# Strict turns between loads and DMA transposes for two batches of a fused attention and mixture-of-experts kernel

## The chip, the core and the metric

The kernel runs on one core of one Trainium2 chip. The metric is the device time of one execution in microseconds. The time before is the median of nine runs. Profiles are one execution each, taken by the hardware profiler; "the span" is the time from the first to the last instruction in it.

Engines as the profile names them: PE is TensorE (PEld its weight loads), DVE is VectorE, ACT is ScalarE, POOL is GpSimd, SP is SyncE. POOL and SP mostly issue DMAs here.

## What is computed

A cosine-weighted linear attention over 8 batches, 8 heads, 576 positions and 64 dimensions, and behind it a layer of 8 experts whose gates are balanced by eight Sinkhorn rounds.

```python
def phi(x, c, s):
    r = np.maximum(x, 0.0)
    return np.concatenate([r * c, r * s], axis=-1)
q_p = phi(q, cos_w, sin_w)
k_p = phi(k, cos_w, sin_w)
kv = np.einsum('bhsf,bhsd->bhfd', k_p, v)
z = np.sum(k_p, axis=2)
num = np.einsum('bhsf,bhfd->bhsd', q_p, kv)
den = np.einsum('bhsf,bhf->bhs', q_p, z)[..., None] + 1e-06
...
logits = x @ w_gate
logits = logits - logits.max()
P = np.exp(logits)
for _ in range(8):
    P /= P.sum(1, keepdims=True) + 1e-09
    P /= P.sum(0, keepdims=True) + 1e-09
    P *= N / E
for e in range(E):
    h = np.maximum(x @ w1[e], 0.0)
    ye = h @ w2[e]
    out += P[:, e:e + 1] * ye
```

Here x is num / den with the heads side by side: 4608 tokens of 512 values.

## The kernel before

The program has two parts. In the first, the attention of the eight batches is woven into the first expert's two matrix products. In the second, the other seven experts follow, in a form with fewer multiplications. The change touches the first part only.

**Blocks and slots.** The first expert's work is cut into blocks j = 0 to 6 of 512 tokens. A block has 16 slots (`NS`). Slots 0 to 7 (`ffn1`) each multiply by one slice of w1 into a bank `h_ps` (two of them) and let ScalarE write the Relu to `hT`. Slots 8 to 15 (`ffn2`) each do half of one row of w2 into `y_ps`, which ScalarE copies to `acc` after every second slot. Behind each slot the program runs what the dictionary `todo` holds for it; `at(j, slot, fn, ...)` puts a step there. Within a slot, steps run in the order in which they were put (lines 668 to 757).

**Attention steps.** In block j, batch b = j + 1 is brought to its end (`sums`, `denominators`, `spread_out`, `numerators`, whose result `xT` the next block reads), and batch b + 1 is prepared:
- `prep_q(b, hk)`: VectorE takes the Relu of a pair of heads' queries in place (`q_ld`), multiplies by the cosines and sines into `q_p` (a pool of three buffers), and, from batch 2 on, SP issues a DMA transpose of `q_p` into one of eight homes: six `q_pT` tiles, a lent piece of `acc_lo`, a lent piece of `acc_hi` (line 361). A batch has four such pairs, hk = 0 to 3.
- `prep_k(b, hk)`: the Relu of the keys in place, on ScalarE in these blocks (line 342).
- `prep_kv(b, hk)`: VectorE multiplies the keys by cosines and sines into `k_p`, and copies v into a home with a column of ones (in `acc_lo`).
- `sums(b, half)`: TensorE multiplies `k_p` with v, 36 matmuls for a half (two pairs).
- `denominators(b)`: TensorE multiplies the turned queries of all four pairs with the key sums; it needs all four transposes.

**Loads.** `load(b, half, names, held_back)` issues one DMA on POOL's queue for each of q, k, v, half a batch each, from 32-bit input to 16-bit tiles (`q_ld`, `k_ld`, `v_ld`, four buffers of each name). With `held_back` it waits for the last VectorE instruction written before it. Six loads bring a batch. The loads of batch 4 are put at slot 12 of block 1, those of batch 5 at slots 11 and 12 of block 2.

**Order.** TensorE, VectorE and ScalarE are wrapped so that each runs its instructions in the written order (`InOrder`, `te`, `ve`, `se`). SP and POOL are not wrapped; the framework places their instructions, and each still issues one after the other. `after(earlier, i)` adds a real wait of i for `earlier`; for a DMA `earlier`, that is its completion. Before the change there is one such wait between loads and transposes: the transpose of (b = 3, hk = 0) waits for the landing of the second half of batch 3's v.

The batches count from zero: the fourth and fifth batch are b = 3 and b = 4. Block 1 prepares b = 3, block 2 prepares b = 4, block 3 prepares b = 5. In the profile TensorE begins block 2 at 66.81 us, block 3 at 87.06 us and block 4 at 106.10 us.

The profile gives line 109 for every operation of the three wrapped engines, so groups there are told apart by their tiles.

Of the kernel before, what the change touches and what calls it, by code (L numbers as in the profile page):

```python
# [25 lines left out]
def kernel(  # L26
# [18 lines left out]
    HK = H // 2  # L45
# [46 lines left out]
    def after(earlier, i):  # L92

        tc.add_manual_dep(
            i.ins,
            earlier.ins.name,
            mybir.DependencyInfo(mybir.DependencyClass.Sync, mybir.DependencyReason.DATA),
            reason="start",
        )
# [81 lines left out]
    with ExitStack() as p1:  # L181
# [11 lines left out]

        loaded = {}
        landing = {}
        sources = {"q": q, "k": k, "v": v}

        def load(b, half, names="qkv", held_back=False):
            for name in names:
                x = ld.tile([P, 2, C, D], F16, name=f"{name}_ld")  # L200
                view = sources[name][b].rearrange("(hk hh) (p c) d -> (hh p) hk (c d)", hh=2, c=C)
                i = nc.gpsimd.dma_start(  # L202
                    out=x[:].rearrange("p hk c d -> p hk (c d)"),
                    in_=view[:, 2 * half : 2 * half + 2],
                )
                if held_back:

                    after(ve.last, i)
                landing[name, b, half] = i
                for i in range(2):  # L210
                    loaded[name, b, 2 * half + i] = x[:, i]
# [20 lines left out]
        for name in "kv":  # L232
            load(0, 0, name)
            load(0, 1, name)
# [111 lines left out]
        def prep_q(b, hk):  # L346

            q16 = loaded.pop(("q", b, hk))
            by_dma = b >= 2
            if by_dma:  # L350
                ve.tensor_scalar(
                    out=q16, in0=q16, scalar1=0.0, scalar2=None, op0=ALU.max
                )
            q_p = qp_pool.tile([P, C, 2, D], F16, name="q_p")
            ve.tensor_tensor(
                out=q_p[:], in0=q16.unsqueeze(2).to_broadcast([P, C, 2, D]),
                in1=cs, op=ALU.mult,
            )
            if by_dma:
                qTs[b, hk] = q_pTs[(b * HK + hk) % len(q_pTs)]  # L360
                turned = nc.sync.dma_start(
                    out=qTs[b, hk], in_=q_p[:].rearrange("p c a d -> p (c a d)"),
                    transpose=True,
                )
                if b == 3 and hk == 0:

                    after(landing["v", b, 1], turned)
            else:
                qps[b, hk] = q_p

# [97 lines left out]
        def sums_made(b, half, kv_ps):  # L468
            kv_sb, zsel = kvs[b]
            W_ = D + 1 if b else D  # L470
            for hh in range(2):
                kv_v = kv_ps[hh][:, 0 : 2 * W_].rearrange("p (hk d) -> p hk d", d=W_)
                se.copy(out=kv_sb[:, 2 * half : 2 * half + 2, hh, :], in_=kv_v[:, :, 0:D])
                if b:
                    ve.tensor_tensor(
                        out=zsel[:, 4 * half + hh : 4 * half + 4 : 2, :],
                        in0=zmask[:, 4 * half + hh : 4 * half + 4 : 2, :],
                        in1=kv_v[:, :, D : D + 1].to_broadcast([P, 2, 32]),
                        op=ALU.mult,
                    )  # L480
# [123 lines left out]
        def at(block, slot, fn, *args):  # L604
            todo.setdefault((block, slot), []).append((fn, args))
# [59 lines left out]
        for hk in range(3):  # L665
            prep_q(1, hk)

        for j in range(B):
            b = j + 1
            if j == 0:  # L670

                def sums_first(half):
                    sums_made(1, half, sums_begun(1, half))

                for hk in range(HK):
                    for i in range(3):
                        at(0, (5, 6, 6, 7)[hk], turn, 1, hk, i, i != 1)
                    if hk == 0:
                        at(0, 5, prep_q, 1, 3)
                    if hk == 2:  # L680
                        at(0, 6, prep_v, 1, 0, se.copy)
                        at(0, 6, prep_v, 1, 2, ve.tensor_copy)
                    if hk == 3:
                        at(0, 7, prep_v, 1, 1, se.copy)
                        at(0, 7, prep_v, 1, 3, ve.tensor_copy)
                for half in range(2):
                    at(0, 7, sums_first, half)
                at(0, 8, denominators, 1)
                at(0, 10, gates, 0)
                for hk in range(HK):  # L690
                    at(0, 11 + hk, attend, 1, hk)
            elif b < B:
                if j == 1:
                    at(0, 13, load, b + 1, 0, "q", True)
                    for hk in range(HK):
                        if hk >= 2:
                            at(j, 0, prep_k, b, hk, False)
                        at(j, 0, prep_kp, b, hk)
                        at(
                            j, (0, 0, 1, 3)[hk], prep_v, b, hk,  # L700
                            (ve.tensor_copy, se.copy)[hk // 2],
                        )
                    for name, half in (("q", 1), ("k", 0), ("k", 1), ("v", 0), ("v", 1)):
                        at(j, 0, load, b + 1, half, name, True)
                    at(j, 3, sums, b, 0)
                    at(j, 5, sums, b, 1)
                elif j == 2:
                    at(j, 0, sums, b, 1)
                else:
                    at(j, 0, prep_kv, b, 2)  # L710
                    at(j, 1, prep_kv, b, 3)
                    at(j, 2, sums, b, 0)
                    at(j, 2, sums, b, 1)
                at(j, 6 if j == 1 else 3 if j == 2 else 4, denominators, b)
                for hk in range(HK):
                    if j == 1:
                        at(j, (9, 10, 12, 13)[hk], attend, b, hk)
                    else:
                        at(j, (7, 8, 10, 11)[hk], spread_out, b, hk)
                if j > 1:  # L720
                    at(j, 9, numerators_of, b, 0, 1)
                    at(j, 13, numerators_of, b, 2, 3)
            if j:
                at(j, 5, gates, j)
            if j == 0:
                for half in range(2):
                    at(j, 3, load, b + 1, half)
                for slot, fn, hk, *args in (
                    (8, prep_q, 0), (11, prep_k, 0), (12, prep_q, 1), (12, prep_k, 1),
                    (13, prep_q, 2), (14, prep_q, 3),  # L730
                ):
                    at(j, slot, fn, b + 1, hk, *args)
            elif b + 1 < B:
                for slot, fn, hk in (
                    (4, prep_q, 0), (5, prep_q, 1), (8, prep_k, 0), (8, prep_q, 2),
                    (9, prep_k, 1), (10, prep_kv, 0), (10, prep_k, 2), (12, prep_q, 3),
                    (12, prep_kv, 1), (12, prep_k, 3), (13, prep_kv, 2), (14, prep_kp, 3),
                    (14, prep_v, 3),
                ) if j == 1 else (
                    (4, prep_q, 0), (5, prep_k, 0), (5, prep_q, 1), (6, prep_k, 1),  # L740
                    (8, prep_q, 2), (8, prep_k, 2), (10, prep_q, 3), (10, prep_k, 3),
                    (11, prep_kv, 0), (14, prep_kv, 1),
                ) if j == 2 else (
                    (3, prep_k, 0), (4, prep_k, 1), (5, prep_q, 0), (6, prep_q, 1),
                    (7, prep_k, 2), (8, prep_q, 2), (10, prep_q, 3), (10, prep_k, 3),
                    (11, prep_kv, 0), (14, prep_kv, 1),
                ):
                    at(j, slot, fn, b + 1, hk, *((se.copy,) if fn is prep_v else ()))
                if j == 1:
                    at(j, 15, sums, b + 1, 0)  # L750
            if j == 1:
                for name in "qkv":
                    for half in range(2):
                        at(j, 12, load, b + 2, half, name, True)
            elif j and b + 2 < B:
                for half in range(2):
                    at(j, 11 + half, load, b + 2, half, "qkv", True)
# [490 lines left out]
    while stream:  # L1248
        _, pair, name = stream.pop(0)
# [32 lines left out]
```

The softmax here doesn't subtract the row's maximum and nothing guards it: scores larger than these inputs give would overflow.

## Time and profile before

| what | value |
|---|---|
| median of nine runs | 978.71 us (977.74 to 979.42) |
| the profiled execution | 978.71 us |
| its span | 977.0 us |
| granted TensorE clock | 1.00 |
| TensorE busy in block 2 (66.81 to 87.06 us) | 18.89 of 20.25 us |
| TensorE busy in block 3 (87.06 to 106.10 us) | 19.04 of 19.04 us |
| a transpose, issue on SP | about 1.3 us |
| a transpose, issue to landing | 3.2 to 9.9 us |
| a load of half a batch, issue on POOL | about 0.72 us |
| median to landing: q, k, v loads | 6.7, 8.7, 9.8 us |

Times in a timeline are from the start of the span. A line has the start, the duration, the engine, the line of the source, the operation, the written and the read tile with their shapes, and the count of merged instructions; in square brackets stands how long the engine was idle just before, and what ended that. For a DMA the duration is that of its issue; when the data has landed is told by the view of DMA issues, in which the last number of a line is the median time from issue to landing.

### The profile page before, as it was taken

What the parts mean: (1) busy time and instruction counts of PE and PEld (TensorE: products, weight loads), DVE (VectorE), ACT (ScalarE), POOL (GpSimd) and SP (SyncE); (2) the same over time, 40 slices, a digit from 0 to 9 for tenths busy, and PEclk for the clock granted to TensorE, in tenths of its full rate; (3) what the DMA queues carried; (4) which work ended last, traced back from release to release, by engine and by line L of the source; (5) the groups of instructions that cost most, each with busy time, mean ns of one, the idle gap of its engine ahead of it and who ended that gap; (6) DMA issues with size and microseconds to landing.
All of it is one profiled execution on the core that took longest, in us unless ns stands there. A gap on an engine that the chain in (4) does not pass through costs nothing.

```text
span 977.0 us, 20236 instructions
## 1 busy us (share of the span) xinstructions
PE 962.5 (99%) x7855; PEld 675.5 (69%) x7855; DVE 808.0 (83%) x1833; ACT 563.6 (58%) x1262; POOL 60.7 (6%) x82
## 2 busy tenths in 40 slices
PE   9999999999999999999999999999999999999997
PEld 6545555457777777777777777777777777777775
DVE  6767775888988887988888887988888888988887
ACT  5766665477776555555555555555555555555551
POOL 6231110010000000000000000000000000000001
PEclk9999999999999999999999999999999999999999
DMA  9999985330104401323103401323103401104435
GB/s 163 184 153 174 152 141 111 68 68 34 42 25 84 77 25 41 64 53 68 34 25 84 77 25 39 65 53 65 38 25 80 81 25 37 38 26 121 127 89 128
DMA packets 80336, 73.54 MB, mean 75 GB/s; under 512 B 33264, under 2 KB 72176, under 8 KB 80240
## 3 DMA queue, kind: packets, MB, share of 16 engines
q0 software_dynamic: 27232, 30.94, 20.2%
q1 hardware_dynamic: 52768, 41.06, 17.3%
q8 instruction: 61, 1.00, 0.4%
q14 instruction: 35, 0.29, 0.1%
q10 hardware_dynamic: 240, 0.26, 0.1%
HBM read 83.12 MB, written 12.98 MB: 98 GB/s over the span
## 4 chain that ended last, share of the span: by engine, by line
PE 88%; DMA 5%; DVE 3%; issue 2%; ACT 1%; POOL 1%; POOLq 0%; ACTq 0%; SPq 0%
PE rows_ps L109 33%; PE h_ps L109 26%; PE p_ps L109 11%; PE copied_ps L109 11%; PE y_ps L109 4%; PE small_ps L109 2%; DMA k_ld<-in_k_dram 1%; DMA w1e<-in_moe_w_dram 1%; DMA w2e<-in_moe_w_dram 1%; DMA acc_hi<-q_p 1%; DVE P_tok L109 1%; DVE colp L109 0%; POOL q_ld L202 0%; DVE rs L109 0%; DVE acc_hi L955 0%
## 5 line engine op out<-in xcount | busy, mean ns | idle before, releaser
L955 DVE SCALAR_TENSOR_TENSOR acc_lo<-rows_ps,P_tok,acc_lo 128x512 f32<-128x512 f32 (+1 forms) x322 | 203.5, 641 | 74.9 <-PE rows_ps L109 74.8
L109 PEld LDWEIGHTS <-H 128*128 128x128 f16 x2080 | 203.1, 98 | 82.5 <-issue 1.2
L891 ACT CAST u<-h_ps 128x384 f16<-128x384 f32 x288 | 137.5, 478 | 131.3 <-PE h_ps L109 131.3
L109 PEld LDWEIGHTS <-w1e 128*128 128x128 f16 x1632 | 157.7, 98 | 67.6 <-issue 5.2
L885 DVE CUSTOM_DVE_ANT_0 H<-p_ps,u 128x384 f16<-128x384 f32 x329 | 181.3, 551 | 6.5 <-PE p_ps L109 6.5
L109 PEld LDWEIGHTS <-hs 128*128 128x128 f16 x1500 | 146.6, 98 | 56.2
L109 PE MATMUL h_ps<-S,w1e 128*128 128x384 f16 x672 | 164.1, 326 | 0.7 <-ACT u L109 0.6
L109 PE MATMUL p_ps<-xT,T 128*128 128x384 f16 x672 | 164.1, 326 | 0.1
L109 PE MATMUL rows_ps<-V,H 128*128 128x256 f16 x1000 | 150.0, 273 | 0.7 <-DVE acc_hi L955 0.7
L109 PE MATMUL rows_ps<-w2e,hs 128*128 128x256 f16 x1000 | 150.0, 273 | 0.0
L109 PE MATMUL h_ps<-xT,w1e 128*128 128x384 f16 (+1 forms) x616 | 148.7, 350 | 0.1
L923 ACT ACTIVATE H<-h_ps 128x384 f16<-128x384 f32 x144 | 70.6, 490 | 95.1 <-PE h_ps L109 95.1
L109 PEld LDWEIGHTS <-T 128*128 128x128 f16 x1008 | 98.4, 98 | 30.2 <-issue 3.6
L109 PE MATMUL rows_ps<-w2e,H 128*128 128x256 f16 (+1 forms) x568 | 92.3, 285 | 0.0
L904 ACT COPY copied_ps<-h_ps 128x384 f32<-128x384 f32 x144 | 67.5, 469 | 35.5 <-PE h_ps L109 35.5
L914 ACT ACTIVATE H<-copied_ps 128x384 f16<-128x384 f32 x144 | 70.8, 492 | 20.4 <-PE copied_ps L109 20.4
L109 PE MATMUL h_ps<-S,T 128*128 128x384 f16 x336 | 81.8, 324 | 0.5 <-ACT copied_ps L109 0.3
L109 PE MATMUL copied_ps<-xT,w1e 128*128 128x384 f16 x336 | 82.1, 326 | 0.0
L109 PE MATMUL copied_ps<-w2e,H 128*128 128x256 f16 x504 | 75.5, 272 | 0.0
L109 PE MATMUL rows_ps<-V,hs 128*128 128x256 f16 x500 | 75.0, 272 | 0.0
L955 DVE SCALAR_TENSOR_TENSOR acc_lo<-copied_ps,P_tok,acc_lo 128x256 f32<-128x256 f32 x126 | 60.2, 478 | 0.6 <-PE copied_ps L109 0.2
L955 DVE SCALAR_TENSOR_TENSOR acc_hi<-rows_ps,P_tok,acc_hi 128x512 f32<-128x512 f32 (+1 forms) x56 | 41.3, 738 | 20.5 <-PE rows_ps L109 19.7
(145 smaller groups left out, 949.9 us busy)
## 6 DMA issues: line engine op xcount, KB each, us to landing
S<-x_saved SPq DMA_DIRECT2D x108, 192.0 KB, 2.4
out_dram<-acc_lo SPq DMA_DIRECT2D x62, 128.0 KB, 2.4
w1e<-in_moe_w_dram POOLq DMA_DIRECT2D x7, 1024.0 KB, 8.8
w2e<-in_moe_w_dram POOLq DMA_DIRECT2D x7, 1024.0 KB, 9.6
q_ld<-in_q_dram POOLq DMA_DIRECT2D x16, 288.0 KB, 6.7
k_ld<-in_k_dram POOLq DMA_DIRECT2D x16, 288.0 KB, 8.7
v_ld<-in_v_dram POOLq DMA_DIRECT2D x16, 288.0 KB, 9.8
x_saved<-S SPq DMA_DIRECT2D x18, 192.0 KB, 1.9
```

The costliest lines, as they stand in the source:

```text
L109: i = getattr(self.engine, name)(*args, **kwargs)
L885: latest = ve._custom_dve(TENSOR_ADD_SAT, out=out, in0=ps[:, 0:TU], in1=t[:], s0=FP32_MAX, s1=0.0)
L891: se.copy(out=t[:], in_=ps[:, 0:TU])
L904: se.copy(out=Y[:, 0:TU], in_=X[:, 0:TU])
L914: se.activation(out=h11, in_=Y[:, 0:TU], func=AF.Relu)
L923: se.activation(out=h12, in_=X[:, 0:TU], func=AF.Relu)
L955: ve.scalar_tensor_tensor(out=a, in0=rows, scalar=P_tok[:, g, self.e : self.e + 1], in1=a, op0=ALU.mult, op1=ALU.add,)
```

## The change

Two kinds of waits are added, and the steps of block 2 get other slots.

- All four transposes of batches 3 and 4 wait for the landing of the second half of their batch's v. Before, only (3, 0) did.
- `turnings` remembers each transpose. The loads of batch 4 wait for the completion of the transpose (3, 3), and those of batch 5 for that of (4, 3), in place of the wait for VectorE's last instruction. The loads of batch 5 are put at slot 14 of block 2 instead of 11 and 12.
- In block 2 the preparation of batch 4 moves: `prep_q` from slots 4, 5, 8, 10 to 6, 7, 9, 14; `prep_k` from 5, 6, 8, 10 to 9, 10, 11, 12; `prep_kv` of pair 0 from 11 to 13; that of pair 1 stays at 14, now behind `prep_q` of pair 3.
- Block 3, which prepares batch 5, and all later blocks keep their slots; so do the loads of batch 6 and 7.

```diff
@@ def load
-        def load(b, half, names="qkv", held_back=False):
+        def load(b, half, names="qkv", held_back=False, behind=None):
...
-                if held_back:
+                if behind is not None:
+
+                    after(turnings[behind], i)
+                elif held_back:
 
                     after(ve.last, i)
@@ def prep_q
-                if b == 3 and hk == 0:
+                if b in (3, 4):
 
                     after(landing["v", b, 1], turned)
+                turnings[b, hk] = turned
@@ the steps of block 2
-                    (4, prep_q, 0), (5, prep_k, 0), (5, prep_q, 1), (6, prep_k, 1),
-                    (8, prep_q, 2), (8, prep_k, 2), (10, prep_q, 3), (10, prep_k, 3),
-                    (11, prep_kv, 0), (14, prep_kv, 1),
+                    (6, prep_q, 0), (7, prep_q, 1), (9, prep_k, 0), (9, prep_q, 2),
+                    (10, prep_k, 1), (11, prep_k, 2), (12, prep_k, 3), (13, prep_kv, 0),
+                    (14, prep_q, 3), (14, prep_kv, 1),
                 ) if j == 2 else (
@@ the loads of the batch after next
             if j == 1:
                 for name in "qkv":
                     for half in range(2):
-                        at(j, 12, load, b + 2, half, name, True)
+                        at(j, 12, load, b + 2, half, name, True, (b + 1, HK - 1))
+            elif j == 2:
+                for half in range(2):
+                    at(j, 14, load, b + 2, half, "qkv", True, (b + 1, HK - 1))
             elif j and b + 2 < B:
                 for half in range(2):
                     at(j, 11 + half, load, b + 2, half, "qkv", True)
```

More of the change, by code (lines that the diff above doesn't have):

```diff
@@ L195 @@
         landing = {}
+        turnings = {}
         sources = {"q": q, "k": k, "v": v}
-        def load(b, half, names="qkv", held_back=False):
+        def load(b, half, names="qkv", held_back=False, behind=None):
             for name in names:
```

## The prediction

> **What bounds the kernel now.** I read the page first: TensorE is busy 99% of the span. So a microsecond that it loses is lost for good, and the change can give back only what TensorE idles around it. The windows view confines that: the stretch 58.60 to 78.30 us has 1.65 us of idle TensorE, the next three have none.
>
> ```profile
> PE 962.5 (99%) x7855; PEld 675.5 (69%) x7855; DVE 808.0 (83%) x1833; ACT 563.6 (58%) x1262; POOL 60.7 (6%) x82
> 58.60:78.30 19.70, 18.05 (x194) 8.96 (x192) 12.99 (x30) 12.68 (x30) 4.31 (x6) 1.00 1.08 167
> 78.30:97.20 18.90, 18.90 (x208) 9.87 (x207) 13.26 (x32) 13.11 (x31) 4.31 (x6) 1.00 1.06 170
> ```
>
> (Columns: stretch, its length, PE, PEld, DVE, ACT, POOL busy with counts, clock, DMA share, GB/s.) Then the timelines of SP and TensorE for the fourth batch (b = 3), and its landings in the DMA view:
>
> ```profile
> 54.34 2.51 SPq L361 DMA_TRANSPOSE q_pT<-q_p  x1
> 63.59 1.29 SPq L361 DMA_TRANSPOSE q_pT<-q_p  x1
> 64.99 1.31 SPq L361 DMA_TRANSPOSE acc_lo<-q_p  x1
> 66.47 1.46 SPq L361 DMA_TRANSPOSE acc_hi<-q_p  x1
> ...
> acc_hi<-q_p SPq DMA_TRANSPOSE x1, 6.9
> ...
> 73.42 0.34 PE L109 MATMUL small_ps<-acc_hi,zsel 128*32 128x192 f16 x6 [1.06 <-DMA acc_hi<-q_p]
> ```
>
> The last transpose of b = 3 goes out at 66.47, beside the loads of b = 4 (66.43 to 70.74), lands after 6.9 us, and TensorE waits 1.06 us. Transposes with no load beside them (97.33, 98.73, 100.17, 102.16) land in 3.2 to 3.4 us. That wait is what can be won. One transpose of b = 3 left at 54.34, before the v loads had landed (53.77 + 8.3 and 54.5 + 9.1), though the code makes hk = 0 wait: the order on SP was hk 1 first, and hk 0 at 63.59.
>
> Next, the consumers of b = 4 and 5, from the POOL, ACT, DVE and TensorE timelines:
>
> ```profile
> 84.25 0.72 POOL L202 DMA_DIRECT2D q_ld<-in_q_dram  x1 [13.51 <-DVE acc_lo L109]
> 84.96 0.72 POOL L202 DMA_DIRECT2D k_ld<-in_k_dram  x1
> ...
> 92.61 0.67 ACT L109 ACTIVATE k_ld<-k_ld 128x576 f16<-128x576 f16 x1
> 93.19 0.59 ACT L109 ACTIVATE hT<-h_ps 128x512 f16<-128x512 f32 x1
> ...
> 85.18 1.55 DVE L109 TENSOR_TENSOR xT<-small_ps,rb 128x384 f16<-128x384 f32 x4 [1.23 <-PE small_ps L109]
> 86.65 0.75 DVE L109 TENSOR_TENSOR k_p<-k_ld,acc_hi 128x1152 f16<-128x1152 f16 x1
> ...
> 89.37 0.44 DVE L109 COPY acc_lo<-v_ld 128x576 f16<-128x576 f16 x1
> ...
> 89.79 1.32 PE L109 MATMUL small_ps<-acc_lo,k_p 64*128 64x65 f16 x72
> ...
> 95.03 1.89 PE L109 MATMUL h_ps<-xT,w1e 128*128 128x512 f16 x8
> ```
>
> The reader is to see two thin margins: DVE finishes the last v copy of b = 4 at 89.81, just as TensorE begins its sums at 89.79; and ACT takes the first keys of b = 5 at 92.61, which landed at 84.96 + 5.8 = 90.8, only 1.8 us sooner.
>
> [...] so each new wait is for a landing, not an issue. The trace agrees: the transpose at 63.59 starts when v has landed (54.5 + 9.1 = 63.6). [...] here 1.31 us of issue against 3.3 to landing, so I use landings. [...]
>
> **Part 1, b = 3.** All four transposes now wait for the last v, so the one at 54.34 moves behind 63.59. Without it beside them the loads land sooner: six loads with nothing beside them took 12.25 us from first issue to last landing (84.25 to 87.80 + 8.7), about 1.45 each after the first; five issued from 51.64 would end at about 62.4, not 63.6. First transpose 62.5, landing 65.7. Query buffers are three, and DVE's fourth q_p of b = 3 (64.33 now, released by the landing of the transpose of 54.34, 64.24) then starts at 65.8: DVE is 1.45 us late. Behind it stand the k_p and v copies that TensorE's sums at 66.13 to 68.99 already wait for, so TensorE is 1.45 late too. The fourth transpose leaves SP at 62.5 + 3 x 1.4 = 66.8 and lands at 70.0, before TensorE's denominators (71.69 + 1.45): the 1.06 us wait goes. TensorE continues at 73.9 where it did at 73.70: **+0.2 us**. Bounds: -1.1 if DVE's lateness is covered, +1.2 if v lands at 63.6 as now.
>
> **Part 2, loads of b = 4.** POOL waits for that landing, 70.0 for 66.43. Issued q, q, k, k, v, v, they land 1.45 apart from 75.1 to 82.3. Each use moved later (prep_q at slots 6, 7, 9, 14; prep_k at 9 to 12; prep_kv at 13, 14): slot 6 ends near 76.7, slot 9 near 79.9 with k0 landed at 78.0. No wait. Behind the waiting load POOL holds only loads. **0.**
>
> **Part 3, DVE in slots 13 and 14 of block 2.** Relu and q_p of hk 3 (81.82 to 82.83, start to start: 1.01 us) and k_p with v copy of hk 0 (as 86.65 to 87.68: 1.03) move behind the xT multiplications of 85.18 to 86.65. There was room before them (DVE waits 1.23 for TensorE), none behind. The last v copy ends at 89.81 + 2.04 = 91.85. TensorE needs it for the last quarter of its 72 sums (from about 90.73): **+1.1 us**.
>
> **Part 4, transposes of b = 4.** Three leave at 82.4, 83.8, 85.2. The fourth needs q_p of slot 14: 86.65, then k_p and copy 1.03, then 1.01, so 88.7. It leaves at 88.8 and lands at 92.1; denominators are at 92.88 + 1.1, so TensorE does not wait.
>
> **Part 5, loads of b = 5.** They go out at 92.1 in place of 84.25. Their first uses have not moved. Order q, k, v: first keys issue at 92.8, land at +5.8 = 98.6. ACT reaches prep_k(5, 0) at 92.61 + 1.1 = 93.7 and stands still. Behind it is the Relu of slot 4, which frees the h_ps bank of slot 6; TensorE runs on through slot 4, denominators, slot 5 and gates, to 95.03 + 1.1 = 96.15. Keys 98.7, prep_k 0.68, Relu 0.59: TensorE goes on at 99.9: **+3.75**. The next Relu stands behind prep_k(5, 1): ready at 101.0 where slot 6 ends at 100.77: **+0.2**. Then the transposes of b = 5 (from 98.4) run beside these loads; second-half keys, alone due at 94.9 + 8.0 = 102.9, ACT wants at 103.3. Lateness from contention: none if transposes queue behind the loads[...], 1.2 if they slow them as the loads of b = 3. I take **+0.5**.
>
> Sum: 0.2 + 1.1 + 3.75 + 0.2 + 0.5 = 5.75. All later stretches hang on TensorE with no idle time to absorb it. The profiled execution took 978.71 us, span 977.0 and 1.7 around it, equal to the median: 978.71 + 5.75 = 984.5.
>
> **Rivals.** *The turns pay* (not slower): from block 1 only the removed 1.06 us counts, DVE's lateness finding cover, and b = 5 lands in time. For it: contention is real (6.9 against 3.3). Against: loads of b = 5 may start no later than 84.25 + 1.8 = 86.05, so the last transpose of b = 4 must leave by 82.7, and its q_p stands in slot 14, behind an xT multiplication that waits for TensorE until 85.18. Price: 978.71 - 1.1 + 1.1 (part 3) = 978.7; at best 977.6 if part 3 is hidden too. *A turn ends earlier than I think*, the load being released at the issue of the transpose (90.2): keys at 96.7, part 5 falls by 1.9, 982.6; against it the start at 63.59. *The lateness spreads*: contention costs 1.2 for the keys, the fourth transpose of b = 4 contends or lands late and DVE's queries of b = 5 wait as well; parts at their upper ends: 1.2 + 1.5 + 4.8 + 0.2 + 1.2 = 8.9, 987.6. *The change does not do what it says*: for b = 3 it nearly only reorders two transposes; parts 3 and 5 are untouched by this, so it is inside my case.
>
> **How the numbers follow.** Forecast 0.74; earlier release 0.08; spread 0.10; turns pay 0.08, with 0.06 of that within 0.2% and 0.02 below. Low end 981.8: part 1 at -1.1 and part 5 at 2.4 with no contention. High end 987.5, the spread. I count the chance of a smaller stall inside 0.2% (1.96 us, about what a measurement can tell from no change) as 0.01 more: faster 0.02, same 0.07, slower 0.91.
>
> **What would show it.** Fourth transpose of b = 4 landing near 92, loads of b = 5 starting within 0.3 of it; ACT idle about 5 us ahead of a k_ld Relu released by the k_ld DMA; TensorE idle 3 to 4 us there for ACT's hT, and about 1 us ahead of the sums near 91. No TensorE wait for acc_hi<-q_p near 73. Wrong if the loads of b = 5 go out before 87, or if ACT does not wait for k_ld.

## The result, and the profile after

| what | before | after |
|---|---|---|
| median | 978.59 us (29 runs, 977.34 to 981.83) | 985.79 us (9 runs, 984.81 to 987.89) |
| ratio, 95% interval | | 1.0076 (1.0067 to 1.0085) |
| span of the profiled execution | 977.0 us | 984.0 us |
| granted TensorE clock | 1.00 | 0.996 |

The changed kernel is slower by 7.2 us. The instructions of TensorE are the same, in the same order; it waits more and, for a few microseconds, runs at half clock (0.50 from 99.5 to 104.5 us). The timeline of TensorE after:

```profile
67.46 0.46 PE L109 MATMUL small_ps<-acc_lo,k_p 64*128 64x65 f16 x18 [1.26 <-DVE acc_lo L109]
...
73.48 0.34 PE L109 MATMUL small_ps<-acc_hi,zsel 128*32 128x192 f16 x6
73.75 1.90 PE L109 MATMUL h_ps<-xT,w1e 128*128 128x512 f16 x8
...
91.06 0.46 PE L109 MATMUL small_ps<-acc_lo,k_p 64*128 64x65 f16 x18 [0.57 <-DVE acc_lo L109]
92.08 0.46 PE L109 MATMUL small_ps<-acc_lo,k_p 64*128 64x65 f16 x18 [0.57 <-DVE acc_lo L109]
92.48 1.90 PE L109 MATMUL h_ps<-xT,w1e 128*128 128x512 f16 x8
...
99.57 3.57 PE L109 MATMUL h_ps<-xT,w1e 128*128 128x512 f16 x8 [2.98 <-ACT hT L109]
102.94 0.68 PE L109 MATMUL small_ps<-hl,acc_hi 96*128 96x192 f16 x3
103.42 1.91 PE L109 MATMUL y_ps<-w2e,hT 128*128 128x512 f16 x4
...
106.48 0.68 PE L109 MATMUL small_ps<-q_pT,kv_sb 128*64 128x384 f16 x8
```

The wait for the fourth transpose of b = 3 is gone (73.48 shows none); a wait for VectorE's v copy stands before it (67.46). Then come the sums of b = 4, the wait for ScalarE at 99.57, and behind it matmuls that take twice as long: 3.57 us for eight where the kernel before took 1.89 at 95.03.

The timeline of ScalarE after shows what it waited for:

```profile
93.55 0.60 ACT L109 ACTIVATE hT<-h_ps 128x512 f16<-128x512 f32 x1 [0.56 <-PE h_ps L109]
98.35 0.68 ACT L109 ACTIVATE k_ld<-k_ld 128x576 f16<-128x576 f16 x1 [4.21 <-DMA k_ld<-in_k_dram]
98.94 0.58 ACT L109 ACTIVATE hT<-h_ps 128x512 f16<-128x512 f32 x1
...
104.57 0.68 ACT L109 ACTIVATE k_ld<-k_ld 128x576 f16<-128x576 f16 x1 [0.20 <-DMA k_ld<-in_k_dram]
```

The first keys of b = 5 come so late that the Relu of slot 4 (98.94) stands behind them, as the prediction had it. The second half of the keys, taken at 104.57, is late too: it goes out at 95.61 and lands 8.9 us later.

And the timelines of SP and POOL why the keys are late:

```profile
83.14 1.30 SPq L365 DMA_TRANSPOSE q_pT<-q_p  x1
...
89.00 1.27 SPq L365 DMA_TRANSPOSE q_pT<-q_p  x1
...
70.39 1.43 POOL L203 DMA_DIRECT2D q_ld<-in_q_dram  x2 [15.38 <-DMA acc_hi<-q_p]
...
92.77 0.72 POOL L203 DMA_DIRECT2D q_ld<-in_q_dram  x1 [18.08 <-DVE zsel L109]
93.48 0.72 POOL L203 DMA_DIRECT2D k_ld<-in_k_dram  x1
```

The loads of b = 4 begin at 70.39, the transposes of b = 4 at 83.14; the fourth leaves at 89.00 and lands 3.2 us later, at 92.2; the loads of b = 5 go out at 92.77. The releaser named for that wait (zsel) is only the event that came last by the profile; the wait written in the code is for the transpose, and its landing fits: in every run with such a turn the first load goes out 0.53 to 0.57 us after the landing of its transpose. From load to load a batch takes 92.77 - 70.39 = 22.4 us. A block lasts about 19 us (87.06 to 106.10 before). So a full cycle of turns is longer than the block into which it has to fit. It runs only once here, because the loads of b = 6 have no turn.

The windows view of the changed kernel has the clock (columns as before: PE, PEld, DVE, ACT, POOL busy, clock, DMA share, GB/s):

```profile
95.00:96.50 1.50, 1.50 (x30) 0.95 (x25) 1.27 (x2) 0.00 (x0) 1.50 (x3) 1.00 1.18 198
96.50:99.50 3.00, 0.10 (x4) 0.03 (x2) 2.86 (x7) 1.15 (x3) 0.57 (x1) 0.85 1.16 176
99.50:100.50 1.00, 0.93 (x3) 0.37 (x3) 0.20 (x1) 1.00 (x4) 0.00 (x0) 0.50 1.19 185
...
104.50:105.50 1.00, 1.00 (x5) 0.51 (x4) 0.00 (x0) 0.68 (x1) 0.00 (x0) 0.54 1.38 177
105.50:106.50 1.00, 1.00 (x8) 0.34 (x6) 0.00 (x0) 0.70 (x2) 0.00 (x0) 1.00 1.24 227
```

The clock falls to one half late in the 3 us of idle TensorE (0.85 is the mean from 96.5 to 99.5) and comes back near 105.5 (0.54 in the microsecond before, 1.00 in the one after), so about 6 us pass at half speed behind the gap.

### The profile page after: what moved, and what is told of

Read it like the earlier page. It is cut to its first block, busy times and chain, and to the rows that moved or that the text cites. A ratio compares the mean times of both kernels' runs of the same rounds, so it can differ in the third digit from the quotient of the medians.

```text
span 984.0 us, 20239 instructions
## 1 busy us (share of the span) xinstructions
PE 965.5 (98%) x7855; PEld 676.5 (69%) x7855; DVE 807.8 (82%) x1833; ACT 564.0 (57%) x1262; POOL 60.7 (6%) x82
## 4 chain that ended last, share of the span: by engine, by line
PE 88%; DMA 5%; DVE 3%; issue 2%; ACT 1%; POOL 1%; POOLq 0%; ACTq 0%; SPq 0%; DVEq 0%
PE rows_ps L109 33%; PE h_ps L109 26%; PE p_ps L109 11%; PE copied_ps L109 11%; PE y_ps L109 4%; PE small_ps L109 2%; DMA k_ld<-in_k_dram 2%; DMA w1e<-in_moe_w_dram 1%; DMA w2e<-in_moe_w_dram 1%; DVE P_tok L109 1%; DVE colp L109 0%; POOL q_ld L203 0%; DMA q_pT<-q_p 0%; DVE rs L109 0%; DVE acc_hi L963 0%
```

## The experiments

Eleven runs in three rounds. The kernel before was measured again beside each round: 978.74, 978.86 and 978.56 us. Differences below are from the median of the same round; the changed kernel was not run again, its 985.79 is from the first comparison.

### What is behind the wait for the keys

**e1: the turn of the loads of b = 5 taken back.**

```diff
-            elif j == 2:
-                for half in range(2):
-                    at(j, 14, load, b + 2, half, "qkv", True, (b + 1, HK - 1))
             elif j and b + 2 < B:
```

> The changed kernel with one turn taken back: the loads of b = 5 stand at slots 11 and 12 of block 2 again and wait for VectorE's last instruction, not for the transpose (4, 3). My theory: ScalarE's wait for the first keys of b = 5 (4.2 us) and TensorE's wait behind it (3.0 us) go, and with them the half clock after it (2.9 us). What comes instead is the meeting of these loads with the transposes of b = 4 (83.1 to 92.2 us now): the fourth lands after 6 to 8 us instead of 3.2, so 95 to 97, and the denominators at 94.3 wait 1 to 3 us. Total 980 to 983 us. Rival, the keys of b = 5 are not what holds the kernel: 985 to 986 us, with the wait at another place. Rival, the meeting costs nothing: 979.8 us.

Measured: 989.02 us, ratio 1.0106 (1.0084 to 1.0128). Slower than the changed kernel by 3 us, and slower than every case that I had written down. The wait for the keys is gone, as expected (the Relu of the first keys, at 101.66, follows an hT Relu without a pause). The timelines of VectorE and TensorE in this run:

```profile
94.73 0.76 DVE L109 TENSOR_TENSOR q_p<-q_ld,acc_hi 128x1152 f16<-128x1152 f16 x1 [6.86 <-DMA q_pT<-q_p]
...
96.57 0.68 PE L109 MATMUL small_ps<-acc_lo,k_p 64*128 64x65 f16 x18 [6.43 <-DVE acc_lo L109]
```

The first transpose of b = 4 left at 83.89 beside the loads (83.27 to 87.54) and landed after 10.7 us. VectorE's fourth q_p needs its buffer; it stood for 6.86 us with the k_p and v copies behind it. TensorE waited 6.43 us for these, and the clock was at one half from 93.0 to 103.2. I had looked for the harm at the denominators; it came earlier, through the three query buffers. So the turn for b = 5 isn't the fault by itself: given that the transposes of b = 4 start so late, it protects them.

**e2: the gap filled.** Fourteen matmuls of 512 columns whose result nothing reads, behind the gates of block 3 (`keep_busy` counts in quarters of such a matmul, hence 56).

```diff
+        def warm(n):
+            nonlocal idle_ps
+            idle_ps = ps_s.tile([P, 512], FP32, name="small_ps")
+            keep_busy(n)
...
+            if j == 3:
+                at(j, 5, warm, 56)
```

> The changed kernel with 14 matmuls of 128x512 on ones, whose result nothing reads, written on TensorE behind the gates of block 3, where it stands idle for 2.98 us. 14 x 0.216 = 3.0 us, so they fit the gap. Theory: the granted clock of 0.50 from about 99 to 105.5 us comes from that gap; with it filled, the clock stays 1.00, the work of slots 6 to 9 runs at full speed, and the time falls by 2.9 us, to 982.9 us. Rival, the clock falls for another reason[...]: 985.8 us or a little more, with 0.50 again in the same place.

Measured: 985.03 us, ratio 1.0061 (1.0041 to 1.0080): 0.8 us below the changed kernel, not 2.9, and the two intervals overlap. The clock did what the theory said: 1.00 in every window from 95 to 111 us, and eight matmuls of h_ps take 2.08 us. The time did not. The timelines of TensorE and ScalarE:

```profile
97.47 3.21 PE L109 MATMUL small_ps<-ones_sq 128*128 128x512 f16 x14
101.00 2.08 PE L109 MATMUL h_ps<-xT,w1e 128*128 128x512 f16 x8 [0.32 <-ACT hT L109]
...
106.91 0.49 PE L109 MATMUL small_ps<-q_pT,kv_sb 128*64 128x384 f16 x4 [1.24 <-ACT rb L109]
...
105.81 0.68 ACT L109 ACTIVATE k_ld<-k_ld 128x576 f16<-128x576 f16 x1 [1.50 <-DMA k_ld<-in_k_dram]
```

At full speed TensorE meets the next late load, the second half of the keys, which ScalarE takes at 105.81 with a copy of `rb` behind it. The half clock had covered that wait. So the gap causes the half clock: with it filled, all four executions had a mean clock of 0.999 or 1.000, where nine of the ten of the changed kernel had 0.994 to 0.998. The two losses lie over one another, and taking the half clock away alone is worth 0.8 us or nothing. The tenth execution of the changed kernel says the same: it had a clock of 1.000 and took 985.75 us, no less than the median.

**e3: the keys of b = 5 used later.**

```diff
-                    (3, prep_k, 0), (4, prep_k, 1), (5, prep_q, 0), (6, prep_q, 1),
-                    (7, prep_k, 2), (8, prep_q, 2), (10, prep_q, 3), (10, prep_k, 3),
+                    (5, prep_q, 0), (6, prep_q, 1), (7, prep_k, 0), (8, prep_k, 1),
+                    (8, prep_q, 2), (9, prep_k, 2), (10, prep_q, 3), (10, prep_k, 3),
```

> The changed kernel with all its turns, but in block 3 the Relu steps of the keys of b = 5 (prep_k) move from slots 3, 4, 7, 10 to 7, 8, 9, 10. Theory: the loads are as late as before (first keys landing near 98.4 us), but nothing on ScalarE wants them before 99; TensorE's wait of 3.0 us and the half clock behind it (2.9 us) go: 985.8 - 5.9 = 979.9 us. Rival, late loads hurt in any case, through VectorE's queries of b = 5 or contention with the transposes of b = 5: 982 us or more.

Measured: 983.83 us (the runs reach from 981.79 to 986.87), ratio 1.0047 (1.0033 to 1.0061). TensorE's wait for hT is gone; 2 us are won, not 5.9, and the rival was right. The profiled execution, 985.10 us, is one of the slower ones. The timelines of VectorE and TensorE:

```profile
104.02 0.31 DVE L109 TENSOR_SCALAR q_ld<-q_ld 128x576 f16<-128x576 f16 x1 [2.86 <-DMA q_ld<-in_q_dram]
...
105.65 0.51 PE L109 MATMUL small_ps<-hl,acc_hi 96*128 96x192 f16 x3 [2.02 <-DVE xT L109]
```

The second half of the queries holds VectorE, with xT behind it, and TensorE waits for the banks that xT frees; 3.4 us at half clock follow (0.50 from 108 to 110, 0.60 and 0.69 in the microseconds on either side). In the changed kernel VectorE had waited 2.74 us at the same place, and the half clock had covered that.

**e8: the queries later as well.** As e3, with `prep_k` at slots 7, 8, 10, 11 and `prep_q` of pairs 2 and 3 at 10 and 13.

> The changed kernel with all its turns, and in block 3 all uses of the late loads later: prep_k at slots 7, 8, 10, 11 (not 3, 4, 7, 10), prep_q of pairs 2 and 3 at slots 10 and 13 (not 8 and 10), so behind the xT multiplications of slot 9 and 13 on VectorE. Theory: moving only the keys left 2.9 us in which VectorE waited for the second half of the queries with xT behind it; with these moved too, no engine wants a load of b = 5 before it lands, and what is left over before is the lateness of the sums (1.4 us): 980 us, up to 981.5 if the last transpose of b = 5 now meets the loads of b = 6. Rival, late loads cost by their contention with the transposes of b = 5, wherever they are used: 983 us or more.

Measured: 993.43 us, ratio 1.0153 (1.0139 to 1.0167), the slowest of all. No engine waits for a load of b = 5 for longer than 1 us, so that half of the theory holds. What I had put at 1.5 us costs ten. The timeline of TensorE, and the landing of the last transpose of b = 5 in the view of DMA issues:

```profile
120.25 0.51 PE L109 MATMUL small_ps<-acc_lo,zsel 128*32 128x192 f16 x6 [4.52 <-DMA acc_lo<-q_p]
125.59 0.51 PE L109 MATMUL small_ps<-acc_hi,zsel 128*32 128x192 f16 x6 [4.83 <-DMA acc_hi<-q_p]
```

```profile
acc_hi<-q_p SPq DMA_TRANSPOSE x1, 15.7
```

The last two transposes of b = 5 (107.36 and 109.87) now run beside the loads of b = 6 (106.48 to 110.8), which have no turn, and take 12.8 and 15.7 us to land. TensorE waits 9.35 us for the two, and the clock is at one half from 119.8 to 130.0. Part of this meeting is of the edit's own making: it puts `prep_q` of pair 3 at slot 13, behind the slots of the loads of b = 6 (11 and 12), which wait for the VectorE instruction written before them. With the pair at slot 10 these loads go out 1.27 us behind the last transpose (110.84 and 109.57 in the changed kernel, likewise in e3). So e8 shows what a meeting costs, and not what later uses alone would.

### Which part of the change makes the loads late

**e4: VectorE's added work in slot 13 taken ahead of the xT step.**

```diff
-                    (10, prep_k, 1), (11, prep_k, 2), (12, prep_k, 3), (13, prep_kv, 0),
+                    (10, prep_k, 1), (11, prep_k, 2), (12, prep_k, 3), (12, prep_kv, 0),
```

> The changed kernel with prep_kv of pair 0 of b = 4 at slot 12 of block 2 instead of 13, so that VectorE does its 1.03 us ahead of the xT multiplications and not behind them. If losses add up as in my prediction, TensorE's sums of b = 4 come 1.0 us sooner and the time falls by 1.0 us, to 984.8 us. If the later wait for the keys of b = 5 absorbs it (they land near 98.4 us whatever TensorE did before, because the fourth transpose of b = 4 waits for the landing of the first at 88.1 us), TensorE only stands idle a microsecond longer: 985.8 us, same as the changed kernel within 0.5 us, or a little more if the clock stays low for longer.

Measured: 986.24 us, ratio 1.0071 (1.0055 to 1.0087), no gain over the changed kernel. The wait for the keys didn't absorb a gain, for there was none to absorb: the sums of b = 4 end 5.83 us after the start of block 3 (87.57 to 93.40), in the changed kernel 5.53 (86.95 to 92.48). The timeline of VectorE in this run shows why:

```profile
89.11 0.76 DVE L109 TENSOR_TENSOR q_p<-q_ld,acc_hi 128x1152 f16<-128x1152 f16 x1 [1.66 <-DMA q_pT<-q_p]
```

The fourth q_p waits 1.66 us for its buffer (0.31 in the changed kernel), which the landing of the first transpose sets free, and the k_p and v copies for the sums stand behind it. Two limits stood close together; the edit removed one. The loads of b = 5 go out no sooner for it (93.69), and TensorE waits 3.87 us for hT where it waited 2.98. Whether a microsecond won at the sums would be waited away at the keys stays untested.

**e5: the transposes of b = 4 without their wait for v.**

```diff
-                if b in (3, 4):
+                if b == 3:
...
-                    (10, prep_k, 1), (11, prep_k, 2), (12, prep_k, 3), (13, prep_kv, 0),
-                    (14, prep_q, 3), (14, prep_kv, 1),
+                    (10, prep_k, 1), (11, prep_q, 3), (11, prep_k, 2), (12, prep_k, 3),
+                    (12, prep_kv, 0), (14, prep_kv, 1),
```

> The changed kernel without the wait of the transposes of b = 4 for their batch's v; the turns of the loads of b = 4 behind (3, 3) and of b = 5 behind (4, 3) stay. Free of that wait, prep_q of pair 3 of b = 4 goes to slot 11 of block 2 and prep_kv of pair 0 to slot 12. Theory: what makes the loads of b = 5 late is that the turns run one behind the other (transposes, 6 loads of 13 us, transposes, 6 loads of 13 us), above all the transposes of b = 4 that stand behind the v load. Without that, the fourth leaves near 83.5 and lands by 87 even beside the loads, the loads of b = 5 go out near 87, and their first keys land at 92.5 to 93.5, where ScalarE wants them: 978.6 to 980.5 us. Rival, the transposes crawl beside the loads so that the turn for b = 5 is as late as with the wait: 984 us or more.

Measured: 983.40 us, ratio 1.0049 (1.0035 to 1.0062): above my range. The four transposes ran beside the loads of b = 4, with a median of 6.7 us to landing; VectorE waited 2.93 us for the first one's buffer, and the loads of b = 5 went out at 91.37, not near 87. The rival had the mechanism, and its price was 0.6 us too high. The 2.4 us won over the changed kernel go with loads 1.4 us sooner, a wait of 0.52 us for hT in place of 2.98, and no half clock (1.00 in the whole stretch).

**e6: the turn of the loads of b = 4 alone.** The block 2 slots of e5; pair 0 alone of b = 3 waits for v; the loads of b = 5 as before.

```diff
-                        at(j, 12, load, b + 2, half, name, True)
+                        at(j, 12, load, b + 2, half, name, True, (b + 1, HK - 1))
```

> The kernel before with one turn alone: the loads of b = 4 wait for the transpose (3, 3). The other added waits are left out (of the transposes of b = 3 only pair 0 waits for v, the transposes of b = 4 and the loads of b = 5 are free, the latter in their old slots), and block 2 has the slots of the last kernel. Theory: VectorE is not late in block 1, the fourth transpose of b = 3 has no load beside it and lands near 70, the wait of 1.06 us on TensorE goes, and nothing comes in its place: 977.6 us, 1.0 less than before. Rival, the later loads of b = 4 cost something in block 2: 978.6 us or more.

Measured: 980.85 us, ratio 1.0022 (1.0010 to 1.0033). The rival: later loads of b = 4 cost something in block 2. The wait of 1.06 us is gone (TensorE does the denominators of b = 3 at 71.54 to 72.3 without a pause), but the first two transposes of b = 4 meet the delayed loads and need 9.3 and 9.0 us. The timelines of VectorE and TensorE:

```profile
85.40 0.76 DVE L109 TENSOR_TENSOR q_p<-q_ld,acc_hi 128x1152 f16<-128x1152 f16 x1 [3.66 <-DMA q_pT<-q_p]
...
87.71 0.38 PE L109 MATMUL h_ps<-xT,w1e 128*128 128x512 f16 x1 [1.60 <-DVE xT L109]
```

Behind this wait TensorE runs 3.4 us at half clock (89.5 to 92.9). The slots of block 2 differ from those before as well, so the loads alone need not account for all of it.

**e7: the wait of the transposes of b = 4 alone.**

```diff
-                if b == 3 and hk == 0:
+                if b == 3 and hk == 0 or b == 4:
```

> The kernel before with one wait more: all four transposes of b = 4 wait for the landing of the second half of their v. No loads wait for transposes, all slots as before. Theory: v lands near 80, the fourth transpose leaves near 84 and lands by 90 beside the loads of b = 5, before the denominators at 92.9; VectorE waits under 1 us for a query buffer where it has room. So this wait alone costs nothing: 978.7 us, within 0.5. It is dear only where the loads of b = 4 are already late and those of b = 5 wait behind it. Rival, this wait alone is what costs: 981 us or more.

Measured: 979.49 us, ratio 1.0007 (0.9999 to 1.0015). As good as nothing; the median is 0.6 above, at the edge of what can be told. The steps came later than I had put them: v landed at 81.6, VectorE waited 2.27 us for a buffer, the fourth transpose left at 86.07 and landed at 91.3. The denominators (93.86) still didn't wait. The wait becomes dear only in the chain.

**e10: the wait of the transposes of b = 3 alone.**

```diff
-                if b == 3 and hk == 0:
+                if b == 3:
```

> The kernel before with one wait more: all four transposes of b = 3, not pair 0 alone, wait for the landing of the second half of their v. Theory: as part 1 of my prediction. VectorE gets its query buffer 1.3 us later, TensorE's sums of b = 3 come 1.3 us later, but TensorE then finds the fourth transpose landed (it has a start of over 1 us before the loads of b = 4, which wait for VectorE): the wait of 1.06 us goes and the lateness takes its place. Same as before within 0.5 us: 978.3 to 979.3. Rival, the lateness adds to the wait: 980 us.

Measured: 978.90 us, ratio 1.0000 (0.9991 to 1.0009). The fourth transpose lands after 3.2 us, TensorE doesn't wait for it, and waits 0.90 us for the v copy instead (67.43). This is part 1 of the prediction by itself, and it costs nothing that can be told.

**e11: the turn for b = 5 ends at the third transpose.**

```diff
-                    at(j, 14, load, b + 2, half, "qkv", True, (b + 1, HK - 1))
+                    at(j, 14, load, b + 2, half, "qkv", True, (b + 1, HK - 2))
```

> The changed kernel with one word changed: the loads of b = 5 wait for the third transpose of b = 4, (4, 2), which lands near 90.0, not for the fourth, which leaves at 89.0 and lands at 92.2. Theory: the loads go out about 2.7 us sooner, their first keys land near 95.7 instead of 98.4, ScalarE's wait falls from 4.2 to about 1.5 us and TensorE's behind it from 3.0 to under 0.5[...]. The fourth transpose has a start of a microsecond before the loads and lands by 94, as the denominators begin. All in all 980.5 to 982 us. Rival, the fourth transpose crawls behind the loads as those of the run with these loads untied (10 us and more): the denominators wait, 984 us or more.

Measured: 983.42 us, ratio 1.0043 (1.0027 to 1.0060): 2.4 us won by one word, but 1.4 us above the end of my range. The timelines of POOL and TensorE:

```profile
91.34 0.72 POOL L203 DMA_DIRECT2D q_ld<-in_q_dram  x1 [16.17 <-DVE acc_lo L109]
...
98.89 2.08 PE L109 MATMUL h_ps<-xT,w1e 128*128 128x512 f16 x8 [1.41 <-ACT hT L109]
```

The loads go out 1.4 us sooner, though TensorE begins block 3 half a microsecond later in this execution (87.47); TensorE's wait is 1.41 in place of 2.98, and the clock stays at 1.00. The fourth transpose leaves at 89.89, 1.45 us ahead of the loads, and lands in 3.2 us: that head start is enough. In e10 1.18 us were enough as well.

**e9: the loads of b = 4 at slot 15 of block 1, no new wait.** In block 2 `prep_k` at slots 8 to 11, `prep_kv` of pair 0 at 12.

```diff
-                        at(j, 12, load, b + 2, half, name, True)
+                        at(j, 15, load, b + 2, half, name, True)
```

> The kernel before with no new wait: the loads of b = 4 are put at slot 15 of block 1 (not 12) and so go out about 2.5 us later, near 69; in block 2 the Relu steps of the keys of b = 4 stand at slots 8 to 11 (not 5, 6, 8, 10) and prep_kv of pair 0 at 12 (not 11). Theory: the fourth transpose of b = 3 (66.5) [...]lands by 71.5, so TensorE's wait of 1.06 us goes. If the transposes of b = 4 then crawl beside the loads of b = 4 as in the run with one turn only, VectorE stands in slot 10 until about 84 and its xT is late by up to 0.5 us. 977.6 to 978.7 us: a gain of up to 1 us over before. Rival, they crawl as long as there (9 us): 980 us or more.

Measured: 979.25 us, ratio 1.0001 (0.9991 to 1.0011): half a microsecond above my range. The 1.06 us wait went (3.2 us to landing), and no gain can be told. The first two transposes of b = 4 need 7.4 and 7.2 us, and TensorE waits 0.21 us for xT where e6 has 1.60. The loads of b = 4 go out 16.6 us ahead of block 3 here (69.77 and 86.33), 15.4 us in e6 (70.11 and 85.52), so little more than a microsecond seems to lie between no loss and 2 us; the two differ in the slots of block 2 as well. It was the best attempt to have the gain without the chain; no run beat the kernel before.

## Why the prediction was right, and where it was off

The direction, the place and the chain of waits were as predicted; the time, 985.79, lies 1.3 us above the forecast. By its own steps, measured as the added delay of TensorE against the kernel before (the changed execution began the sums of b = 3 0.39 us earlier, 65.74 for 66.13; in other traces this start lies anywhere from 65.56 to 66.84, so a few tenths are chance):

| step | predicted, us | shown by the trace, us |
|---|---|---|
| part 1, b = 3 | +0.2 | +0.44 (73.70 to 73.75, plus 0.39) |
| part 2, loads of b = 4 | 0 | -0.16 (block 3 begins at 86.95, before at 87.06) |
| part 3, sums of b = 4 | +1.1 | +1.54 (91.05 to 92.48, plus 0.11) |
| part 5, first wait for the keys | +3.75 | +3.11 (4.54 at slot 6, less 1.43) |
| part 5, what follows to the numerators | +0.2 and +0.5 | +1.88 and +0.99 (97.00 to 103.42, 99.07 to 106.48) |

The rows on the right add up to 7.8; less the 0.39 at the start, TensorE is 7.4 us late in block 3. The two profiled executions differ by 7.0 in the end, the medians by 7.2.

**Part 1** held to the numbers: first transpose at 62.22 (predicted 62.5), fourth landing at 69.8 (70.0), VectorE late by 1.29 us (1.45). e10 shows it alone at zero. **Parts 2 and 4** held: loads of b = 4 at 70.39 and landed by 83.0, fourth transpose landed at 92.2 (92.1). **Part 3** came out with about the right size, but its reason was only half of it. The fourth q_p stood behind the moved steps and also waited 0.31 us for the first transpose's landing at 88.1; e4 takes the first away and finds the second. I had let the sums and the loads hang on VectorE's slot alone.

**Part 5, first wait.** The first keys landed at 98.3 (98.6), and this is in part luck. They went out 0.7 us later than I had put them (93.48 for 92.8), because I had let the loads start at the very landing of the transpose, within 0.3 us, and 0.57 us pass. They then landed sooner, after 4.85 us and not 5.8. I had taken 5.8 from loads "with nothing beside them", but the last transpose of b = 4 was beside those until 86.3.

**Part 5, what follows,** is the step with the wrong size: "+0.2" and "+0.5" were 2.87 us. Two things went into it. The second half of the keys landed at 104.55 and not at 102.9: it went out 0.7 us late and took 8.9 us for 8.0, beside two transposes of b = 5. And I reckoned each matmul at its duration in the trace before, while in the 3 us of idle TensorE its clock fell to 0.50, and stayed there for about 6 us behind the gap. The trace before could not show this price: the longest gap of TensorE from 50 to 180 us was 1.06 us there, and the clock stayed at 1.00 behind it. e2 parts the two. At full clock TensorE is 5.97 us later than before at slot 6 (101.00 for 95.03) and 7.64 us at the matmuls behind the first numerators (107.33 for 99.69), so without the half clock 1.67 us of it are left, 1.24 us of that in the one wait behind the second keys. By the medians the half clock adds 0.8 us, if anything. In a sum of waits, the term after a stall was thus right only as "late loads or half clock, whichever ends last".

**The rivals.** *The turns pay* is out: e10, e9 and e6 show the 1.06 us wait gone, and none is faster than before beyond its interval. *A turn that ends earlier* is out for the changed kernel (92.77 is after the landing), but e11 shows what it is worth: 2.4 us. *The lateness spreads* came about in part: VectorE waited 2.74 us for the queries of b = 5, and the second keys lost about a microsecond to contention. The fourth transpose of b = 4 did not contend, and the time stayed 1.8 us below this rival's 987.6. e8 shows that more was near, and bigger than the 1.2 us that I had put for contention: its two transposes beside six loads landed after 12.8 and 15.7 us.

**The cause, as the runs leave it.** A transpose issued beside six loads lands late (before: 6.9; e6: 9.3; e1: 10.7; e8: 15.7 us; alone: 3.2). The turns do away with that, and each of the two waits on transposes costs nothing that can be told alone (e7, e10). In a strict chain, however, six loads take 12.6 us (70.39 to 83.0), the transposes of b = 4 another 9.1 (83.14 to 92.2), in which the fourth also stands until its q_p is there (89.00): 22 us and more against a block of 19. The loads of b = 5 come 8.5 us later than before. 4.0 of these are there when the chain begins (70.39 for 66.43), 4.5 come in its one cycle (22.4 us against 17.8 before). Their uses were not moved, and ScalarE and behind it TensorE stand for them. e11, which lets them go one transpose sooner, takes back 2.4 us of the loss. Taking links out (e1, e5, e6) brings a meeting of transposes and loads back at another place; moving the uses meets the next late load (e3) or the next loads (e8). Why a transpose beside loads takes so long was not tried and stays open.

## What to carry to other kernels

Before making two streams of transfers take turns, add up one full cycle of turns, issue, landing and the 0.6 us from landing to next issue included, and compare it with the period in which it must fit: here 22.4 us against 19, though each wait on transposes alone cost nothing that could be told. Look for the limit that stands right behind the one you remove: in e4, e2 and e3 a second one took all or most of what the first gave back. Stalls of TensorE of 1.60, 2.00 and 2.02 us were followed by half clock here, others of 1.64 and 1.96 us were not: where a predicted stall is that long, price the work after it at half clock, and take that or the next late load, whichever ends later.

## What the runs showed of the hardware that was not expected

**The clock.** The length of a gap of TensorE did not tell by itself whether the half clock followed. Gaps of 1.60 us (e6, up to 87.71) and of 2.00 and 2.02 us (e3, up to 68.02 and 105.65) were followed by 0.50; gaps of 1.41 us (e11, up to 98.89), 1.64 us (e5, up to 68.10) and 1.96 us (e4, 66.11 to 68.07) by 1.00. Two lines each from the windows views of e6 and e4 (columns as above):

```profile
89.00:90.00 1.00, 1.00 (x6) 0.36 (x4) 1.00 (x3) 0.75 (x2) 1.00 (x2) 0.76 1.12 119
90.00:91.00 1.00, 1.00 (x4) 0.24 (x2) 1.00 (x3) 0.35 (x1) 0.75 (x2) 0.50 1.16 172
...
66.00:70.00 4.00, 1.71 (x40) 0.91 (x34) 3.77 (x8) 1.18 (x4) 0.00 (x0) 1.00 1.01 193
70.00:75.00 5.00, 4.79 (x75) 2.51 (x70) 1.58 (x7) 2.42 (x6) 4.11 (x6) 1.00 0.59 81
```

In e6, where a second gap of 0.35 us follows (up to 88.44), the clock falls between 89 and 90 us; in e4 it stays at 1.00 from 66 to 75 us, around and behind the longer gap. What decides was not tried and stays open. Executions of one and the same kernel differ as well: mean clocks of the changed kernel go from 0.994 to 1.000, and the three executions at 0.994 took 987.5 to 987.9 us.

**The head start.** A transpose that left at nearly the same time as six loads landed sooner the longer its start before them was: after 6.9 us when it left 0.04 us behind the first load (before, 66.47), after 5.1 us with 0.59 us of start (e7, 67.94), and after 3.2 us with 1.18 us (e10) and 1.45 us (e11). With two earlier transposes still on their way 1.27 us were not enough (before, 121.10: 5.9 us).
